# Column sums of an attention softmax: adding exponential tiles on VectorE ahead of the TensorE sums, in seven of 24 units

## The chip, the cores and the metric

The kernel runs on one core of a Trainium2 chip. Its time is the device time of one execution in microseconds (us); for the kernel before, the median of six runs is 421.89 us (420.82 to 422.49). The engines of the core are TensorE (PE in the profile, its weight loads PEld), VectorE (DVE), ScalarE (ACT), GpSimd (POOL) and SyncE (SP), which here only issues DMAs. Each engine works through its own queue in order and waits on semaphores.

## The reference

```python
def rmsnorm(x, g):
    return x / np.sqrt(np.mean(x * x, axis=-1, keepdims=True) + 1e-06) * g
q_n, k_n = rmsnorm(q, g_q), rmsnorm(k, g_k)          # (8, 12, 448, 64)
scores = (1 / sqrt(64)) * q_n @ k_n.T
attn = softmax(scores)                               # over 448 keys
x = (attn @ v) -> (8 * 448, 768)
h = x @ w_in                                         # (768, 2048)
out = np.maximum(0.01 * h, h) @ w_out                # (2048, 768), fp32
```

Eight batches of twelve heads are attended, and each of the 3584 tokens then passes a two-layer network with a leaky ReLU.

## The kernel before

The attention is done in 24 **units**; a unit is four heads of one batch, so three units make a batch. The four heads of a unit lie as two (`a`) by two (`r`) 64-wide blocks, so that four small matmuls fill the array together. The 448 keys of a unit are seven tiles of 64 (`NS = 7`). For each tile, `qk` (L198) computes the transposed scores with keys on the partitions, and `ex` (L205, its ScalarE row is L214) takes the exponential of 128 x 896 scores into `et[:, t]` in fp16.

A unit runs in four **stages** `d = 0..3` (L927 on) that treat the tiles (0), (1, 2), (3, 4), (5, 6). In each stage the scores and exponentials are issued first. Then comes `fill` (L702), which issues matmul items of the network from a queue, as many as the stage's share of the work allows, with small jobs between them: sums of squares (`prep_ssq`, L155), the norm's factor on ScalarE (`prep_rinv`, L160 and L161), the normalised q and k on VectorE (`prep_norm`, L167), and the DMA transpose of the unit after next (`prep_trd`). An item is 1.1 to 1.3 us of matmuls. The first layer (`moe1`, row L362) is evacuated by ScalarE (L356), the second (`moe2`, L403, and `seven`, L444) by VectorE (L407, L451, L460) with sums of activations on VectorE beside it (`s1` to `s4`, L425 to L434).

The softmax's denominators need a sum over keys, that is over partitions and over the seven tiles. TensorE makes it by matmuls with a matrix of ones, accumulating over the tiles in PSUM. From unit 4 to unit 22 (`narrow`, L696) this is `zcol` (L276): 28 matmuls with a 128 x 32 stationary matrix, 224 columns each, four side by side. The last unit uses `zsum_slot` (L268) with 28 matmuls of 64 x 64 by 448 columns. The sums of unit u - 1 are made in stage 0 of unit u, in this order on TensorE: score tile 0 of u, `pv` (values times exponentials) of u - 1, `zcol` of u - 1, `shift_mm` of u. `shift_mm` (L239) is a part of the maximum by which the exponentials are shifted: VectorE reduces tile 0 (L232), makes a diagonal `dg` (L234), TensorE spreads it (L244), VectorE reduces again (L245) and writes the bias `eb` (L253) that the first `ex` needs.

After `zcol`, ScalarE takes a logarithm (`zcol_ln`, L300) and an exponential of its negative (`zcol_inv`, L305), four DMAs on SP's queue broadcast the reciprocals into `rz` (L310), and the attention's result `x32`, copied from PSUM by ScalarE (`pv_out`, L295), is multiplied by `rz` into `xt` (L320). GpSimd does this product (`xmul_pool`) in stage 1 of the next unit, VectorE (`xmul_sb`) for units 4 to 6. `x32`, `rz` and `zs` have one buffer each. In the last unit the product of unit 22 stands in stage 2 on GpSimd, and after the loop come `zsum_slot`, `pv`, `zinv` (L326, L327, which also writes `rz`) and the product L349, then the last batch's network items.

The order on every engine is the order of the code (`manual_schedule`): nothing is rearranged.

Of the kernel before, what the change touches and what calls it, by code (L numbers as in the profile page):

```python
# [8 lines left out]
FP32 = mybir.dt.float32  # L9
FP16 = mybir.dt.float16  # L10
AF = mybir.ActivationFunctionType
ALU = mybir.AluOpType
# [6 lines left out]
def kernel(  # L19
# [11 lines left out]
    nc = tc.nc  # L31

    B, H, S, D = q.shape
    QH = 4
    NS = 7
    P = 128
    NQ = H // QH
    NU = B * NQ
# [6 lines left out]
    cst = ctx.enter_context(tc.tile_pool(name="cst", bufs=1))  # L45
# [4 lines left out]
    zpool = ctx.enter_context(tc.tile_pool(name="zpool", bufs=1))  # L50
# [6 lines left out]
    def aux(shape, dtype, name):  # L57
        if held:
            return held[0].pop(0)
        return psum.tile(shape, dtype, tag="aux", bufs=4, name=name)  # L60
# [6 lines left out]
    def drop(bank):  # L67
        if held:
            held[0].append(bank)
# [3 lines left out]
    ones16 = cst.tile([P, D], FP16)  # L73
    nc.vector.memset(ones16, 1.0)
    onesr = cst.tile([P, 32], FP16)
# [6 lines left out]
    nc.vector.memset(eps_t, 1.0e-6)  # L82
    one32 = cst.tile([1, 1], FP32)
    nc.vector.memset(one32, 1.0)
    grow = cst.tile([1, 2, D], FP32)
    gdup = cst.tile([1, 2, D], FP32)
    gcol = cst.tile([P, 1], FP32)
    gate_t = cst.tile([P, 1], FP16)
    vts = [cst.tile([P, 2, NS, D], FP16, name=f"vt{i}") for i in range(NV)]
# [21 lines left out]
    st = {}  # L111
# [77 lines left out]
    def slot():  # L189
        return psum.tile([P, 2, 512], FP32, tag="sT", bufs=2, name="sT")  # L190
# [7 lines left out]
    def qk(u, steps):  # L198
        st[u]["sT"] = []
        for t in steps:  # L200
            sT = slot()
            score(u, t, (sT[:, 0], sT[:, 1]))
            st[u]["sT"].append((t, sT))
# [17 lines left out]
    def shift_max(u):  # L221
        s = st[u]
        sT = s["sT"][0][1]
        if isinstance(sT, list):
            pm2 = small.tile([P, 2], FP32, tag="pm2", name="pm2")
            for a in range(2):
                nc.vector.tensor_reduce(pm2[:, a:a + 1], sT[a][:, 0:S], axis=AXL.X, op=ALU.max)
            s["spare"] = sT[0]
            nc.vector.tensor_reduce(s["spare"][:, 511:512], pm2, axis=AXL.X, op=ALU.max)
        else:  # L230
            s["spare"] = sT[:, 0]
            nc.vector.tensor_reduce(s["spare"][:, 511:512], sT[:, :, 0:S], axis=AXL.XY, op=ALU.max)  # L232
        s["dg"] = small.tile([P, P], FP16, tag="dg", name="dg")
        nc.vector.tensor_tensor(s["dg"], ident16, s["spare"][:, 511:512].broadcast_to([P, P]), op=ALU.mult)  # L234
# [20 lines left out]
    def gate(u):  # L255
        nc.gpsimd.tensor_copy(gate_t, buf(u, "n16")[:, 1, NS - 1, 1, D - 1:D])
# [3 lines left out]
    def zsum(u, t0=0, t1=NS):  # L260
        s = st[u]
        for t in range(t0, t1):
            for r in range(2):
                for a in range(2):
                    nc.tensor.matmul(s["zt"][r][64 * a:64 * a + 64, 0:S], ones16[64 * r:64 * r + 64],
                                     s["et"][64 * r:64 * r + 64, t, a], start=(t == 0), stop=(t == NS - 1))

    def zsum_slot(u):  # L268
        s = st[u]
        s["zslot"] = slot()  # L270
        s["zt"] = [s["zslot"][:, r] for r in range(2)]
        zsum(u)

    HS = S // 2

    def zcol(u):  # L276
        s = st[u]
        s["zc"] = aux([P, 512], FP32, "zc")
        for t in range(NS):
            for y in range(2):  # L280
                for a in range(2):
                    c = 32 * (2 * y + a)
                    nc.tensor.matmul(s["zc"][c:c + 32, 0:HS], onesr, s["et"][:, t, a, HS * y:HS * y + HS],  # L283
                                     start=(t == 0), stop=(t == NS - 1))

    def pv_slot(u):
        s = st[u]
        s["pslot"] = slot()
        s["pv"] = [s["pslot"][:, r] for r in range(2)]
        pv(u)  # L290

    def pv_out(u):
        s = st[u]
        s["x32"] = zpool.tile([P, 2, S], FP32, tag="x32", name="x32")
        nc.scalar.copy(s["x32"], s["pslot"][:, :, 0:S])  # L295

    def zcol_ln(u):
        s = st[u]
        s["zs"] = zpool.tile([P, HS], FP32, tag="zs", name="zs")
        nc.scalar.activation(s["zs"], s["zc"][:, 0:HS], AF.Ln)  # L300
        drop(s["zc"])

    def zcol_inv(u):
# [3 lines left out]
        for r in range(2):  # L307
            for y in range(2):
                src = s["zs"][64 * y + r:64 * y + 64:2, None, :]
                nc.sync.dma_start(s["rz"][:, r, HS * y:HS * y + HS], src.broadcast_to([32, 4, HS]))  # L310

    def xmul_sb(u):
        xmul_pool(u, nc.vector)

    def xmul_pool(u, eng=nc.gpsimd):
        s = st[u]
        b, g = divmod(u, NQ)
        if b not in xts:
            xts[b] = xpool.tile([P, NQ, 2, S], FP16, tag="xt", name="xt")
        eng.tensor_tensor(xts[b][:, g], s["x32"], s["rz"], op=ALU.mult)  # L320
# [375 lines left out]
    def narrow(u):  # L696
        return 4 <= u < NU - 1
# [46 lines left out]
    with tc.manual_schedule():  # L744
# [182 lines left out]
        for u in range(3, NU):  # L927
            for d in range(4):
                if d > 0 or u > 3:
                    qk(u, STEPS[d])  # L930
                    if d == 0:
                        shift_max(u)
                        if u == 6:
                            xmul_sb(u - 2)
                        if narrow(u - 1):
                            pv_slot(u - 1)
                            zcol(u - 1)
                            shift_mm(u)
                            pv_out(u - 1)
                        else:  # L940
                            zsum_slot(u - 1)
                            pv(u - 1)
                            shift_mm(u)
                            zinv(u - 1)
                    ex(u)
                    if d == 0 and narrow(u - 1):
                        zcol_ln(u - 1)
                jobs = []

                def job(fn, *args):  # L950
                    jobs.append(lambda: fn(*args))

                if d == 0:
                    if u == 3:
                        prep_norm(4)
                        gate(4)
                    elif narrow(u - 1):
                        if u < NU - 1:
                            job(zcol_inv, u - 1)
                    else:  # L960
                        xmul(u - 1)
                    if u + 4 < NU:
                        job(load, u + 4)
                    if u + 3 < NU:
                        load_v(u + 3)
                    if u < 6:
                        prep_sqp(u + 3)
                if d == 1 and narrow(u - 1) and not 5 <= u < 8 and u < NU - 1:
                    xmul_pool(u - 1)
                if u == NU - 1:  # L970
                    if d == 1:
                        job(zcol_inv, u - 1)
                    if d == 2:
                        xmul_pool(u - 1)
                if fed(u, d) and u > 3:
                    push(u // NQ - 1)
                if (u, d) in ((3, 1), (4, 0)):
                    for ti in range(2):
                        prep_tr(u + 1, ti, VV)
                if d == 1 and 5 <= u < NU - 1:  # L980
                    job(prep_g, u + 1)
                if u + 2 < NU:
                    if d == 1:
                        for ti in range(2):
                            job(prep_ssq, u + 2, ALL, (ti,))
                    if d == 2:
                        job(prep_rinv, u + 2)
                        for ti in range(2):
                            job(prep_norm, u + 2, ALL, (ti,))
                        if u > 3:  # L990
                            job(prep_trd, u + 2)
                if d == 1 and 4 <= u < 8:
                    job(weight_sum, u - 4, 0)
                if d == 0 and 5 <= u < 9:
                    job(weight_sum, u - 5, 1)
                if d == 2 and 6 <= u < 8:
                    job(xmul_sb, u - 1)
                if u == NU - 2 and d == 0:
                    for n, tile_ in ((1, (raws, "rq", 3)), (2, (raws, "rk", 3)), (3, None), (4, (prep_p, "sq", 3))):
                        job(win_sum, n, 1, tile_)  # L1000
                    for n in (3, 1, 2, 4):
                        job(x_sum, LATE, n)
                if d == 3 and 6 <= u < NU - 3:
                    for ti in range(2):
                        job(prep_sq, u + 3, ALL, (ti,))
                fill(u, d, jobs)
# [4 lines left out]
        for i, ns in enumerate(((3, 1), (2, 4))):  # L1011
            c, fn = queue[i]
# [33 lines left out]
```

## Time and profile before

| | |
|---|---|
| median of 6 runs | 421.89 us (420.82 to 422.49) |
| profiled execution | 421.53 us, of which the span is 419.8 us |
| granted TensorE clock | 0.994 |
| PE busy | 404.1 us, 96% |
| DVE busy | 270.6 us, 64% |
| ACT busy | 303.9 us, 72% |
| POOL busy | 83.0 us, 20% |
| sums of exponentials, L283 (19 units) | 15.4 us for 504 recorded matmuls |
| products `xt<-x,rz`, L320 | 16 on POOL, 2083 ns each; 3 on DVE, 1087 ns each |

The profile is of one execution. A row of its groups names line, engine, operation, tiles out<-in, shape, count, then the busy time with the mean of one in ns, and the idle time before them with what ended it. Matmuls that run side by side are each counted with their own duration, so the time of a group of them is read from the chain of waits or the timeline (start, duration, engine, line), not from the mean.

### The profile page before, as it was taken

Reading aid. Unit: us, or ns where it says so; the run is one execution under the profiler, and the core shown is the slowest. Engines: PE = TensorE matmul, PEld = TensorE weight load, DVE = VectorE, ACT = ScalarE, POOL = GpSimd, SP = SyncE. Lnnn points to the kernel's source line nnn. Section 1 sums busy time; section 2 is a strip of 40 time slices with the busy share of each in tenths; the row PEclk is TensorE's granted clock in tenths of the full one; section 3 lists DMA queues with packets and bytes.
Section 4 is the critical chain, followed back from the end, with each engine's and each line's share of the span. In section 5 each row is a group of like instructions: output and inputs, shape, how many; then the busy total and the mean of one; then the engine's idle time right before and its main releaser. Section 6 shows DMA issues by size and latency. Waiting matters only on the chain.

```text
span 419.8 us, 9568 instructions
## 1 busy us (share of the span) xinstructions
PE 404.1 (96%) x3959; PEld 222.6 (53%) x3959; DVE 270.6 (64%) x440; ACT 303.9 (72%) x474; POOL 83.0 (20%) x75
## 2 busy tenths in 40 slices
PE   7878999999999999999999999999999999999995
PEld 6544454455445444555455544455445557558863
DVE  5888675887668836566448735467338787527762
ACT  5999877768887689767986779967986657653600
POOL 1867432200020112210121121120101101010000
PEclk9899999999999999999999999999999999999999
DMA  7999999889764796678665796578552460032023
GB/s 268 216 239 241 238 250 147 210 153 212 151 155 81 205 206 134 164 167 179 154 135 98 200 202 146 155 140 165 185 108 44 121 157 9 8 76 75 2 53 99
DMA packets 71951, 62.42 MB, mean 149 GB/s; under 512 B 36324, under 2 KB 67044, under 8 KB 71908
## 3 DMA queue, kind: packets, MB, share of 16 engines
q1 hardware_dynamic: 61312, 49.62, 47.0%
q0 software_dynamic: 10272, 11.80, 18.1%
q8 instruction: 31, 0.51, 0.5%
q10 hardware_dynamic: 324, 0.39, 0.3%
q14 instruction: 12, 0.10, 0.1%
HBM read 45.61 MB, written 11.01 MB: 135 GB/s over the span
## 4 chain that ended last, share of the span: by engine, by line
PE 80%; ACT 9%; DVE 6%; issue 2%; DMA 1%; SPq 0%; DVEq 0%; ACTq 0%
PE hps L362 27%; PE sT L195 8%; ACT et L214 6%; PE sT L340 6%; PE ma L444 5%; PE bank L444 5%; PE md L444 5%; PE bank L564 4%; PE mc L444 4%; PE op L403 3%; PE zc L283 3%; PE mb L444 3%; DVE n L167 2%; PE sT L444 2%; PE bank L403 1%
## 5 line engine op out<-in xcount | busy, mean ns | idle before, releaser
L214 ACT ACTIVATE et<-sT,eb 128x896 f16<-128x896 f32 x166 | 159.6, 1011 | 18.5 <-PE sT L195 16.8
L362 PE MATMUL hps<-xt,win 128*128 128x448 f16 x600 | 120.8, 353 | 0.2 <-DVE xt L349 0.2
L362 PEld LDWEIGHTS <-win 128*128 128x128 f16 x612 | 56.8, 98 | 58.2 <-issue 9.6
L320 POOL TENSOR_TENSOR xt<-x,rz 128x896 f16<-128x896 f32 x16 | 33.3, 2083 | 149.7 <-DMA rz<-zs 141.8
L167 DVE TENSOR_TENSOR n<-rq,rinv 128x896 f16<-128x896 f32 (+2 forms) x25 | 28.5, 1143 | 49.4 <-ACT rinv L161 46.6
L356 ACT ACTIVATE gt<-hps 128x448 f16<-128x448 f32 x100 | 54.1, 557 | 5.9 <-PE hps L362 5.4
L195 PE MATMUL sT<-qkT 64*64 64x448 f16 x664 | 52.8, 366 | 3.3 <-ACT et L214 2.2
L155 DVE TENSOR_REDUCE ssq<-sq 128x14 f32<-128x896 f32 (+2 forms) x49 | 50.5, 1059 | 0.8 <-ACT sq L144 0.6
L444 PEld LDWEIGHTS <-sa 128*128 128x128 f16 x352 | 32.8, 98 | 26.3 <-issue 6.1
L295 ACT COPY x<-sT 128x896 f32<-128x896 f32 x19 | 17.2, 907 | 36.9 <-DVE sT L245 36.9
L124 POOL DMA_DIRECT2D vt<-in_v_dram x24 | 18.2, 759 | 113.8 <-PE sT L340 106.3
L444 PEld LDWEIGHTS <-gt 128*128 128x128 f16 x264 | 25.2, 98 | 19.4 <-issue 2.9
L195 PEld LDWEIGHTS <-qkT 64*64 64x64 f16 x672 | 15.3, 104 | 36.9 <-issue 33.0
L340 PE MATMUL sT<-et,vt 64*64 64x448 f16 x532 | 28.5, 349 | 0.3
L403 PE MATMUL op<-wout,gt 128*128 128x384 f16 x160 | 28.4, 327 | 0.0
L340 PEld LDWEIGHTS <-vt 64*64 64x64 f16 x672 | 20.6, 107 | 12.7 <-issue 1.7
L232 DVE TENSOR_REDUCE sT<-sT 128x1 f32<-128x896 f32 x22 | 24.0, 1093 | 3.5 <-PE sT L195 3.5
L167 DVE TENSOR_TENSOR n<-rk,rinv 128x896 f16<-128x896 f32 (+2 forms) x26 | 26.1, 1011 | 0.0
L403 PEld LDWEIGHTS <-gt 128*128 128x128 f16 x192 | 17.6, 98 | 14.3 <-issue 3.0
L444 PE MATMUL ma<-wout,gt 128*128 128x384 f16 x128 | 23.5, 326 | 0.0
L425 DVE TENSOR_TENSOR sa<-gt 128x512 f16<-128x512 f16 (+1 forms) x15 | 8.2, 545 | 18.5 <-ACT gt L356 13.8
L144 ACT ACTIVATE sq<-rq 128x896 f32<-128x896 f32 (+2 forms) x18 | 16.4, 914 | 1.3 <-DMA rq<-in_q_dram 1.3
(135 smaller groups left out, 516.4 us busy)
## 6 DMA issues: line engine op xcount, KB each, us to landing
rq<-in_q_dram SPq DMA_DIRECT2D x24, 448.0 KB, 3.9
rk<-in_k_dram SPq DMA_DIRECT2D x24, 448.0 KB, 5.7
out_dram<-ost SPq DMA_DIRECT2D x52, 192.0 KB, 3.6
rz<-zs SPq DMA_DIRECT2D x76, 112.0 KB, 2.3
vt<-in_v_dram POOLq DMA_DIRECT2D x24, 224.0 KB, 5.5
win<-in_moe_w_in_dram POOLq DMA_DIRECT2D x8, 384.0 KB, 16.1
wout<-in_moe_w_out_dram POOLq DMA_DIRECT2D x2, 1536.0 KB, 28.4
out_dram<-ost SPq DMA_DIRECT2D x4, 96.0 KB, 2.1
```

The lines of the kernel that those rows point to most:

```text
L124: nc.gpsimd.dma_start(vts[u % NV].rearrange("p a t d -> p a (t d)"), rows(v, u))
L155: nc.vector.tensor_reduce(buf(u, "ssq")[:, ti, :, c[0]:c[1]], buf(u, f"sq{ti}")[:, :, c[0]:c[1]], axis=AXL.X, op=ALU.add)
L167: nc.vector.tensor_tensor(buf(u, "n16")[:, ti, c[0]:c[1]].rearrange("p s a d -> p a s d"), src[:, :, c[0]:c[1]], buf(u, "rinv")[:, ti, :, ...
L195: nc.tensor.matmul(banks[a][64 * r:64 * r + 64, 0:S].rearrange("p (t x) -> p t x", t=NS), kT(u, r, a, t), qT(u, r, a), start=True, stop=True)
L214: nc.scalar.activation(s["et"][:, t], sT[:, :, 0:S], AF.Exp, bias=s["eb"], scale=1.0)
L232: nc.vector.tensor_reduce(s["spare"][:, 511:512], sT[:, :, 0:S], axis=AXL.XY, op=ALU.max)
L320: eng.tensor_tensor(xts[b][:, g], s["x32"], s["rz"], op=ALU.mult)
L340: nc.tensor.matmul(s["pv"][r][64 * a:64 * a + 64, 0:S], vts[u % NV][64 * r:64 * r + 64, a, t], s["et"][64 * r:64 * r + 64, t, a], start=(t ...
L356: nc.scalar.activation(dst, src, AF.Prelu, bias=0.0, scale=1.0, alpha=0.01)
L362: nc.tensor.matmul(hps[:, 0:S], win16[:, kt // 2, kt % 2, ts(ft, P)], xt[:, kt // 2, kt % 2], start=(kt == 0), stop=(kt == KT - 1))
L403: nc.tensor.matmul(op2[:, 0:HC], gt[:, ft, ds(col(t), P)], wout16[:, ft, ds(HC * half, HC)], start=(ft == 0), stop=(ft == FT - 1))
L444: nc.tensor.matmul(bank[:, 0:HC], a[:, f], b[:, f], start=(first and f == 0), stop=(f == HF - 1), skip_group_check=not first)
```

## The change

For units 10, 11, 13, 16, 17 and 19, VectorE adds the exponential tiles 0 to 3 into a new fp16 tile `ea` (three adds), in stage 2 right behind `ex`, and thus ahead of that stage's `fill`. `zcol` then sums tiles 4, 5, 6 and `ea`: 16 matmuls for 28. Behind the adds VectorE takes the product `xt<-x,rz` of the unit before, which GpSimd had in stage 1. For the last unit (23) VectorE adds tiles 0 to 4 (four adds) as a job of stage 3, followed there by the product of unit 22; `zsum_slot` sums tiles 5, 6 and `ea`: 12 matmuls for 28. The two rows of gains (`grow`, `gdup`) that are used only at the start move into the buffer of `x32`; `ea` has one buffer.

```diff
-    grow = cst.tile([1, 2, D], FP32)
-    gdup = cst.tile([1, 2, D], FP32)
+    g_t = zpool.tile([P, 2, S], FP32, tag="x32", name="g_t")
+    grow = g_t[0:1, 0, 0:2 * D].rearrange("p (a d) -> p a d", a=2)
+    gdup = g_t[0:1, 1, 0:2 * D].rearrange("p (a d) -> p a d", a=2)
...
-        zsum(u)
+        ets = z_tiles(u)
+        for i, e in enumerate(ets):
+            for r in range(2):
+                for a in range(2):
+                    nc.tensor.matmul(s["zt"][r][64 * a:64 * a + 64, 0:S], ones16[64 * r:64 * r + 64],
+                                     e[64 * r:64 * r + 64, a], start=(i == 0), stop=(i == len(ets) - 1))
...
+    ADDED = {u: 4 for u in (10, 11, 13, 16, 17, 19)}
+    ADDED[NU - 1] = 5
+
+    def add_e(u):
+        s = st[u]
+        s["ea"] = zpool.tile([P, 2, S], FP16, tag="ea", name="ea")
+        for t in range(1, ADDED[u]):
+            nc.vector.tensor_tensor(s["ea"], s["et"][:, 0] if t == 1 else s["ea"], s["et"][:, t], op=ALU.add)
+
+    def z_tiles(u):
+        s = st[u]
+        ets = [s["et"][:, t] for t in range(NS)]
+        return ets[ADDED[u]:] + [s["ea"]] if "ea" in s else ets
...
-        for t in range(NS):
+        ets = z_tiles(u)
+        for i, e in enumerate(ets):
...
-                    nc.tensor.matmul(s["zc"][c:c + 32, 0:HS], onesr, s["et"][:, t, a, HS * y:HS * y + HS],
-                                     start=(t == 0), stop=(t == NS - 1))
+                    nc.tensor.matmul(s["zc"][c:c + 32, 0:HS], onesr, e[:, a, HS * y:HS * y + HS],
+                                     start=(i == 0), stop=(i == len(ets) - 1))
...
+                if d == 2 and u in ADDED and u < NU - 1:
+                    add_e(u)
+                    xmul_sb(u - 1)
...
-                if d == 1 and narrow(u - 1) and not 5 <= u < 8 and u < NU - 1:
+                if d == 1 and narrow(u - 1) and not 5 <= u < 8 and u not in ADDED:
                     xmul_pool(u - 1)
...
-                    if d == 2:
-                        xmul_pool(u - 1)
...
+                if u == NU - 1 and d == 3:
+                    job(add_e, u)
+                    job(xmul_sb, u - 1)
```

## The prediction

> **What bounds the kernel.** I read three views in this order: the page's busy line and clock, the groups by shape, then the timeline around each place that the change touches.
>
> ```profile
> PE 404.1 (96%) x3959; PEld 222.6 (53%) x3959; DVE 270.6 (64%) x440; ACT 303.9 (72%) x474; POOL 83.0 (20%) x75
> ...
> PEclk9899999999999999999999999999999999999999
> ...
> PE 80%; ACT 9%; DVE 6%; issue 2%; DMA 1%; SPq 0%; DVEq 0%; ACTq 0%
> ```
>
> TensorE is busy 96% of the span at a full granted clock and carries 80% of the chain that ended last. So a microsecond taken off TensorE's queue counts, and one put on VectorE counts only where TensorE then waits for it. The changed units show no ACT or DVE piece in the chain, but for one exp pair in units 11 and 17 (at 173.59 and 269.49).
>
> **What the change removes.** From the instruction listings: 12 matmuls of `zcol` for each of units 10, 11, 13, 16, 17, 19 and 16 of the last `zsum_slot`, each with its weight load; seven GpSimd products. It adds 6 x 3 + 4 adds and seven products on VectorE. ScalarE and the DMAs keep their instructions and order.
>
> ```profile
> L283 PE MATMUL zc<-et,onesr 128*32 128x224 f16 x504 | 15.4, 261 | 0.0
> ...
> L428 DVE TENSOR_TENSOR sa<-sa,gt 128x1024 f16<-128x1024 f16 x7 | 4.8, 682 | 0.0
> ...
> L320 DVE TENSOR_TENSOR xt<-x,rz 128x896 f16<-128x896 f32 x3 | 3.3, 1087 | 0.0
> ```
>
> *Step 1, the column sums.* Four column groups run side by side, so the 261 ns of one matmul is no price. The chain of waits gives one `zcol` (7 tiles, 28 matmuls) 0.79 us up to the next group. In unit 10's (timeline, 161.75) the matmuls run 0.85 us to 162.60 and each takes 0.26, so the last four began at 162.34: six steps in 0.59, 0.098 a tile. The other 0.19 us, up to the following matmul at 162.53, is a foot that stays. Three tiles fewer are worth 3 x 0.098 = 0.295 us. Bounds: 0.28 (half the 0.187 a tile of the 448-wide groups, which take 1.32 for seven) and 0.34 (3/7 of 0.79). I take 0.295, the row itself.
>
> The Trainium skill (TensorEngine Tiling (Array Packing), Key Properties) speaks against counting 3/7 of the group: changing the tiling mode drains TensorE, however few matmuls stand between two changes. The 0.19 us foot agrees with it; 3/7 of 0.79 would give 0.27 us more over six groups than the foot allows.
>
> *Step 2, the matmul behind them.* After `zcol` TensorE runs `shift_mm`, which needs `dg` (L234) from VectorE. The shorter `zcol` is worth its time only if `dg` is done.
>
> ```profile
> 175.17 0.56 DVE L407 COPY ost<-op 128x384 f32<-128x384 f32 x1
> 175.65 0.69 DVE L428 TENSOR_TENSOR sa<-sa,gt 128x1024 f16<-128x1024 f16 x1
> 176.25 1.09 DVE L232 TENSOR_REDUCE sT<-sT 128x1 f32<-128x896 f32 x1
> 177.38 0.29 DVE L234 TENSOR_TENSOR dg<-ident,sT 128x128 f16<-128x128 f16 x1
> ```
>
> These are VectorE's rows (start, duration) around the sum of unit 11, which runs in unit 12, with `zcol` on TensorE from 177.00. `dg` ends at 177.67 and `shift_mm` starts at 177.79; with a wake-up of 0.05 only 0.07 us can be gained, and VectorE then sets it. Unit 17 is alike (`dg` ends 273.56, matmul 273.68). The others have room: unit 10 (162.13, 162.53), 13 (210.30, 210.80), 16 (257.93, 258.43), 19 (306.20, 306.69), at least 0.40 for 0.295. So 4 x 0.295 + 2 x 0.07 = 1.32 us. Bounds for the two: 0.05 and 0.34.
>
> *Step 3, the adds and products inside the units.* No row shows an add of 896 fp16 values with this layout. Between the groups of 672 (L550, 502 ns) and 1024 fp16 values (L428, 682 ns) it is 617 ns, an estimate; bounds 502, and 1087 from the product with fp32 inputs of this size. I take 0.62. The first two adds run in VectorE's gap while it waits for `rinv`; the third waits for the exp of tile 3, the first of a pair on ScalarE. Behind it in the queue stand the product (1.09) and `prep_norm`.
>
> ```profile
> 202.03 1.90 ACT L214 ACTIVATE et<-sT,eb 128x896 f16<-128x896 f32 x2
> ...
> 204.86 1.09 DVE L167 TENSOR_TENSOR n<-rq,rinv 128x896 f16<-128x896 f32 x1 [6.29 <-ACT rinv L161]
> ...
> 208.88 1.10 DVE L232 TENSOR_REDUCE sT<-sT 128x1 f32<-128x896 f32 x1 [0.46 <-PE sT L195]
> ```
>
> Unit 13: exp of tile 3 ends 202.03 + 1.01 = 203.04; add to 203.69; product to 204.78 (its `rz` landed by 201.83, when GpSimd started on it). The norm starts at 204.86 as before: 0.08 us to spare. The same sum gives 172.28 against 172.36 in unit 11, 253.54 against 253.62 in 16, 268.17 against 268.25 in 17, 300.68 against 300.75 in 19. So the cover is VectorE's wait for `rinv` (37.4 us over the middle of the trace). If it were gone, each 0.1 us late reaches L232; units 13 and 19 absorb 0.46 there, 16 absorbs 0.79, while 11 and 17 pass it all on. Cost taken: nothing. No PSUM evacuation stands behind the wait in units 10, 13, 16 and 19 (`hps` goes to ScalarE); in 11 and 17 one does, L407, after the norms.
>
> ```profile
> 156.77 2.07 POOL L320 TENSOR_TENSOR xt<-x,rz 128x896 f16<-128x896 f32 x1 [8.51 <-DMA rz<-zs]
> ...
> 157.73 2.07 DVE L167 TENSOR_TENSOR n<-rq,rinv 128x896 f16<-128x896 f32 x1 [6.20 <-ACT rinv L161]
> ```
>
> Unit 10 is the exception: `rz` lands at 156.77, so the product ends at 157.86 and the norm starts 0.13 late. But its 2.07 us here, against 1.09 elsewhere, ran beside GpSimd's product, which is now gone; the two norms end near 159.95 instead of 160.80, ahead of the score at 160.61. Nothing on the path.
>
> The Trainium skill (SBUF — State Buffer, Who interferes with whom) says that a VectorE instruction with two SBUF inputs contends with a GpSimd instruction that reads SBUF. The doubled row agrees. By it the change takes a collision away and makes none, as GpSimd has no product in these units; in the sum neither moves TensorE.
>
> The moved product has readers only three or more stages later (`push` of its batch), and frees `x32` and `rz` two stages before they are written again. SP's `rz` transfers and ScalarE's copy now wait for VectorE in GpSimd's place, long after; GpSimd's queue only empties.
>
> *Step 4, the last unit.*
>
> ```profile
> 370.88 0.56 DVE L451 TENSOR_TENSOR ost<-bank,ost 128x384 f32<-128x384 f32 x1 [0.74 <-PE bank L444]
> 374.09 0.56 DVE L451 TENSOR_TENSOR ost<-bank,ost 128x384 f32<-128x384 f32 x1 [2.65 <-PE bank L444]
> ```
>
> Seven tiles of 64x64 sums (`zsum_slot`, L265, 374.05 to 375.50 in the chain) become three: 4 x 0.187 = 0.75 us (bounds 0.56, three tiles' worth, and 4/7 of 1.45 = 0.83). The listing puts the adds behind the first of these two VectorE rows, in the idle stretch of 2.65 us before the second: 371.47 + 4 x 0.62 + 3 x 0.04 = 374.07. TensorE first takes tiles 5 and 6 (374.05 to 374.42) and so has the sum in time, by 0.35. The product then runs to 375.16; L326 writes its `rz` buffer and waits for it, so it starts at 375.2 instead of 375.60 (L326's row), gaining 0.4 where TensorE gains 0.75. VectorE's chain of L349 and L550 rows up to 381.4 is then 0.35 late against TensorE; the matmul that needs it first, at 382.97, has 1 us of room. Full 0.75.
>
> **Sum.** 1.32 + 0.75 = 2.07 us. The profiled execution took 421.53 us (span 419.8 and 1.7 around it): 419.46. It lies 0.36 under the median of the runs, 421.89; on that scale the forecast is **419.8 us**, 0.5% faster. With the bounds of steps 1 and 4 and the runs' spread its own range is 419.2 to 420.6. (A measurement here can tell about 0.2% from no change: 421.05 and 422.73.)
>
> **Rivals.**
>
> *B, everything counts:* `dg` comes earlier in units 12 and 18 too and the foot shrinks with the group: 6 x 0.34 + 0.83 = 2.87, 419.0. For it: L232 is only third in a row of VectorE work there. Against it: L407 ahead of it waits for TensorE itself.
>
> *C, fp16 adds at the fp32 rate (1.09 each):* norms 0.4 late. Units 13, 16 and 19 absorb it, 10 too (4 x 0.295 gained); 11 and 17 lose 0.28 each; in the last unit the sum ends at 375.95, TensorE waits and ends 0.8 later. -1.18 + 0.56 + 0.8 = +0.2: 422.1, no change. Against it: all fp16 rows from SBUF run at half the fp32 price.
>
> *D, slower, VectorE becomes the bound at the change of unit:* the moved product takes 2.07 instead of 1.09, as the one collided norm did. Place: in front of `prep_norm` in the stage of tiles 3 and 4. It is then 0.9 late: `dg` of units 12 and 18 comes at 178.54 and TensorE loses 0.80 each; 13 and 19 keep 0.03 of their gain, 10 keeps 0.12, 16 all; in the last unit L326 starts 0.65 later than before and TensorE later waits 0.5, leaving 0.25. 1.60 - 0.06 - 0.12 - 0.295 - 0.25 = +0.9: 422.8. It decides from about 0.5 us of lateness. Against it: GpSimd has nothing to read then.
>
> **Chances.** Forecast 0.62, B 0.15, C 0.12, D 0.11. Faster by over 0.2% is A and B, 0.77; within it C, 0.12; slower D, 0.11. The range 418.8 to 421.9 takes in A, B and the milder half of C.
>
> **What would show it.** Right: `zcol` pieces near 0.50 us in six units; `ea` adds near 0.62; norms of the six units still released by `rinv`; `shift_mm` of units 12 and 18 starting right behind `dg`; L265 near 0.56. Wrong: norms starting after VectorE's own product, a TensorE wait for `ea` in the last sum, or adds near 1.09. A VectorE row other than `dg` in front of TensorE in units 10 to 20 would break step 3.

## The result and the profile after

The changed kernel takes 419.89 us (median of 17 runs, 419.01 to 422.45) against 421.93 of the kernel before (36 runs): a ratio of 0.9956, 95% interval 0.9946 to 0.9967. The forecast was 419.8. Its profiled execution took 419.89 us, 1.64 less than that of before, with a span of 418.1.

Line numbers shift in the changed kernel: by 1 up to the sums and by 20 behind them (21 in the experiments on the last unit's product), so that the product L320 is L340 there, L349 is L369 and L407 is L427. The adds are L288.

On the page of the changed kernel, the busy line and the chain by engine:

```profile
PE 400.7 (96%) x3871; PEld 220.3 (53%) x3871; DVE 290.1 (69%) x469; ACT 303.9 (73%) x474; POOL 68.5 (16%) x68
...
PE 79%; ACT 9%; DVE 8%; issue 2%; DMA 1%; SPq 0%; DVEq 0%; ACTq 0%
```

The reader sees 88 matmuls fewer on PE, 19.5 us more work on DVE, 14.5 us less on POOL, and a chain that has gained 2% of DVE. The new pieces of VectorE in the chain stand at three places: from L427 to `dg` at the sums of units 11 and 17 (175.12 to 177.62 and 270.35 to 272.85), and at L369 and L471 in the last unit (376.08 to 377.72).

VectorE in unit 11 of the changed kernel (start, duration, engine, line, then the idle time before it and who ended it):

```profile
170.50 0.63 DVE L288 TENSOR_TENSOR ea<-ea,et 128x896 f16<-128x896 f16 x1 [1.32 <-ACT et L215]
171.04 1.08 DVE L340 TENSOR_TENSOR xt<-x,rz 128x896 f16<-128x896 f32 x1
172.30 1.09 DVE L168 TENSOR_TENSOR n<-rq,rinv 128x896 f16<-128x896 f32 x1 [0.17 <-ACT rinv L162]
```

The last add waits 1.32 us for its exponential, the product follows, and the norm is still released by `rinv` after 0.17 us of waiting. So the work lies inside the old gap. In five of the six units the norm waits 0.17 us; in unit 17 the product waits 0.24 us for its `rz` and the norm follows it at once, released by VectorE's own product and no longer by `rinv`.

TensorE at the sums of the same unit:

```profile
176.94 0.47 PE L303 MATMUL zc<-et,onesr 128*32 128x224 f16 x12
177.24 0.27 PE L303 MATMUL zc<-ea,onesr 128*32 128x224 f16 x4
177.66 0.22 PE L245 MATMUL sT<-dg,onesp 128*128 128x64 f16 x2
```

VectorE just ahead of it:

```profile
175.12 0.56 DVE L427 COPY ost<-op 128x384 f32<-128x384 f32 x1
175.59 0.68 DVE L448 TENSOR_TENSOR sa<-sa,gt 128x1024 f16<-128x1024 f16 x1
176.19 1.09 DVE L233 TENSOR_REDUCE sT<-sT 128x1 f32<-128x896 f32 x1
177.32 0.29 DVE L235 TENSOR_TENSOR dg<-ident,sT 128x128 f16<-128x128 f16 x1
```

`dg` ran from 177.32 to 177.61, so `shift_mm` started 0.05 us behind it and 0.42 behind the start of the last tile. In unit 10 this last distance is 0.20, which is the foot of 0.19 seen before:

```profile
162.28 0.27 PE L303 MATMUL zc<-ea,onesr 128*32 128x224 f16 x4
162.48 0.23 PE L245 MATMUL sT<-dg,onesp 128*128 128x64 f16 x2
```

To compare kernels stage by stage I take the time from one start of `shift_mm` on TensorE to the next, each time from the stage 0 of a unit to that of the following one, from the timelines. The units from 12 to 21 that are not listed agree within 0.02 us in these five kernels.

| from `shift_mm` of unit to the next, us | before | change | adds only | product twice | s2 later |
|---|---|---|---|---|---|
| 10 | 14.62 | 14.35 | 14.34 | 14.34 | 14.34 |
| 11 | 15.26 | 15.18 | 15.43 | 15.83 | 14.97 |
| 13 | 16.90 | 16.61 | 16.61 | 16.77 | 16.61 |
| 16 | 15.93 | 15.65 | 15.64 | 15.64 | 15.64 |
| 17 | 15.25 | 15.18 | 15.60 | 16.06 | 14.97 |
| 19 | 16.89 | 16.61 | 16.61 | 16.79 | 16.61 |
| gained in the six | | 1.27 | 0.62 | -0.58 | 1.71 |
| last unit, sums to `pv` | 1.35 | 0.60 | 1.12 | 0.59 | 0.59 |
| `pv` to the last batch's first matmul | 5.34 | 5.57 | 5.36 | 5.57 | 5.57 |

The change gains 1.27 in the six units and 0.75 - 0.23 = 0.52 in the last, 1.79 us in all, in the middle of what the ratio's interval allows (1.4 to 2.3 us). The 1.64 us between the two profiled executions is this less some 0.2 us by which the changed kernel's was already late when the first changed unit began (`shift_mm` at 148.13 against 147.91). That start says nothing of the change: in the eight kernels here that have the same code up to there it lies between 147.32 and 148.88, which is why single executions are compared by stage.

### The profile page after: what moved, and what is told of

Read it like the earlier page. It is cut to its first block, busy times and chain, and to the rows that moved or that the text cites. A ratio compares the mean times of both kernels' runs of the same rounds, so it can differ in the third digit from the quotient of the medians.

```text
span 418.1 us, 9413 instructions
## 1 busy us (share of the span) xinstructions
PE 400.7 (96%) x3871; PEld 220.3 (53%) x3871; DVE 290.1 (69%) x469; ACT 303.9 (73%) x474; POOL 68.5 (16%) x68
## 4 chain that ended last, share of the span: by engine, by line
PE 79%; ACT 9%; DVE 8%; issue 2%; DMA 1%; SPq 0%; DVEq 0%; ACTq 0%
PE hps L382 27%; PE sT L196 8%; PE sT L360 5%; PE ma L464 5%; ACT et L215 5%; PE md L464 5%; PE bank L584 4%; PE mc L464 4%; PE bank L464 4%; PE op L423 4%; PE mb L464 3%; PE zc L303 3%; DVE n L168 2%; PE sT L464 2%; PE bank L423 1%
## 5 line engine op out<-in xcount | busy, mean ns | idle before, releaser
L168 DVE TENSOR_TENSOR n<-rq,rinv 128x896 f16<-128x896 f32 (+2 forms) x25 | 27.4, 1098 | 13.8 <-ACT rinv L162 11.0
L340 POOL TENSOR_TENSOR xt<-x,rz 128x896 f16<-128x896 f32 x9 | 19.0, 2116 | 81.4 <-DMA rz<-zs 81.4
L288 DVE TENSOR_TENSOR ea<-ea,et 128x896 f16<-128x896 f16 x15 | 9.4, 626 | 13.6 <-ACT et L215 13.3
```

The lines of the kernel that those rows point to most:

```text
L168: nc.vector.tensor_tensor(buf(u, "n16")[:, ti, c[0]:c[1]].rearrange("p s a d -> p a s d"), src[:, :, c[0]:c[1]], buf(u, "rinv")[:, ti, :, ...
```

## The experiments

The theory: the gain is TensorE's removed matmuls, as far as VectorE's rows do not take their place. The rivals: GpSimd's relief is the gain; TensorE's count alone decides.

| | time, us | ratio to before | 95% interval |
|---|---|---|---|
| the change | 419.89 | 0.9956 | 0.9946 to 0.9967 |
| products only | 421.68 | 0.9996 | 0.9981 to 1.0011 |
| adds only | 421.11 | 0.9974 | 0.9960 to 0.9988 |
| six units only | 420.43 | 0.9962 | 0.9949 to 0.9974 |
| last unit only | 421.48 | 0.9989 | 0.9976 to 1.0001 |
| product twice | 421.44 | 0.9998 | 0.9985 to 1.0012 |
| twelve units | 427.85 | 1.0161 | 1.0131 to 1.0191 |
| s2 later | 419.34 | 0.9938 | 0.9925 to 0.9951 |
| product first | 419.68 | 0.9953 | 0.9940 to 0.9965 |
| both repairs | 418.86 | 0.9938 | 0.9926 to 0.9950 |
| s2 later, no adds | 421.38 | 1.0005 | 0.9991 to 1.0019 |

Each ratio is to runs of the kernel before on the same chip.

**Products only.** The adds go, the moved products stay.

```diff
-                    add_e(u)
                     xmul_sb(u - 1)
...
-                    job(add_e, u)
                     job(xmul_sb, u - 1)
```

> The seven products go to VectorE as in the change, but nothing is added: TensorE keeps all its column-sum matmuls. Theory (the gain is TensorE's removed matmuls): none of the 2.07 us, 421.9 us, ratio 1.000, between 0.998 and 1.002; unit 10's norm falls from 2.07 to 1.09 us and nobody gains by it. Rival (the gain is GpSimd's relief, its products no longer beside VectorE's): most of the 2 us, 420.0 us, ratio 0.9955.

No gain: 0.9996. The collision in unit 10 is gone, as the norm's row in the timeline shows:

```profile
157.46 1.09 DVE L168 TENSOR_TENSOR n<-rq,rinv 128x896 f16<-128x896 f32 x1
```

It took 2.07 us before. VectorE then waits 0.79 us for the score, so nobody needed the 0.98. GpSimd's relief as such is worth nothing that the interval (0.9981 to 1.0011) can tell, nor is the move of `grow` and `gdup`, which this kernel has too.

**Adds only.** The adds stay, the products go back to GpSimd.

```diff
                     add_e(u)
-                    xmul_sb(u - 1)
...
-                if d == 1 and narrow(u - 1) and not 5 <= u < 8 and u not in ADDED:
+                if d == 1 and narrow(u - 1) and not 5 <= u < 8 and u < NU - 1:
                     xmul_pool(u - 1)
...
+                    if d == 2:
+                        xmul_pool(u - 1)
...
                     job(add_e, u)
-                    job(xmul_sb, u - 1)
```

> The adds of the change without its products: GpSimd keeps all 16, so they run at about 2.1 us beside VectorE's work again. Theory: the six units keep 1.3 us, the last unit keeps 0.75, and the last L326 no longer waits for VectorE's product, so that the 0.25 us lost behind it comes back, unless GpSimd's product slows the adds beside it: 419.5 to 420.1 us, ratio 0.9945 to 0.9960. Rival (GpSimd's relief is the gain): 421.9, ratio 1.000. Second rival (the product was moved because it collides with the adds on the path): 420.8 or more.

0.9974: neither my range nor the first rival, but the second, which gives the collision as the reason. In unit 11 GpSimd's product runs from 169.48 to 171.55, and VectorE's third add runs beside it:

```profile
169.48 2.07 POOL L340 TENSOR_TENSOR xt<-x,rz 128x896 f16<-128x896 f32 x1 [7.17 <-DMA rz<-zs]
...
169.69 2.34 DVE L288 TENSOR_TENSOR ea<-ea,et 128x896 f16<-128x896 f16 x1 [1.27 <-ACT et L215]
```

Alone the add takes 0.63. It ends at 172.03, 0.48 after the product: it hardly moved while the product ran. The norm starts at 171.96, behind the add instead of at `rinv`, and unit 11 is 0.17 us longer than before. In unit 17, 0.35 us longer, it is the norm that collides (1.72 us for 1.09). In units 10, 13, 16 and 19 rows collide too, but the table shows `shift_mm` no later there than in the change. In the last unit the first of the four adds takes 1.32 beside GpSimd's product, and TensorE waits for the sum:

```profile
372.74 0.57 PE L277 MATMUL sT<-et,ones 64*64 64x448 f16 x8
373.67 0.38 PE L277 MATMUL sT<-ea,ones 64*64 64x448 f16 x4 [0.36 <-DVE ea L288]
```

The two starts lie 0.93 apart, 0.41 in the change. So the product's move is no gain by itself but what lets the adds pay: with it 1.79 us, without it 0.62 + 0.23 - 0.02 = 0.83.

The Trainium skill (SBUF — State Buffer, Who interferes with whom) has the rule: a VectorE instruction with two SBUF inputs contends with a GpSimd instruction that reads SBUF. These rows agree, and give the price.

**Six units only** and **last unit only.** Each keeps one half of `ADDED`.

```diff
-    ADDED[NU - 1] = 5
```
```diff
-    ADDED = {u: 4 for u in (10, 11, 13, 16, 17, 19)}
+    ADDED = {}
```

> The change in units 10, 11, 13, 16, 17, 19 alone; the last unit as before. Theory: 4 x 0.295 + 2 x 0.07 = 1.3 us, 420.6 us, ratio 0.997; the matmul of shift_mm comes 0.28 earlier after the sums of units 10, 13, 16 and 19 and 0.07 after 11 and 17. Rival (every unit gives its three tiles): 6 x 0.34 = 2.0 us, 419.9, ratio 0.995.

> The change in the last unit alone. Theory: TensorE saves 0.75 us in the sum and loses 0.25 behind it, where the last md matmuls wait for a VectorE row that stands behind the product that waits for the reciprocal: 0.5 us net, 421.4 us, ratio 0.9988. Rival (the last unit gives 0.75 whole): 421.15, ratio 0.9982; in the trace, no TensorE gap behind the second item after the sum.

0.9962 and 0.9989. The interval of the second reaches 1.0001, so by its time alone it isn't clear that the last unit gains. In the timelines the six units gain the same 0.27, 0.08, 0.29, 0.28, 0.07 and 0.28 without the last, and the last has its 0.59 and 5.57 us without the six: the parts add up.

**Product twice.** The six units take the moved product a second time, with the same operands and result.

```diff
                     add_e(u)
                     xmul_sb(u - 1)
+                    xmul_sb(u - 1)
```

> In the six units VectorE takes the moved product twice, to the same tile: 1.0 us more behind the third add. Theory (VectorE's wait for rinv covers the work with 0.1 to 0.2 us to spare, and what exceeds it passes to dg): norms start about 0.85 us later in all six; units 11 and 17 lose 0.85 each, 13 and 19 have 0.46 ahead of L232 and little behind, lose their 0.28 and a little more, 10 and 16 lose little; in all 2.3 to 3.2 us against the change: 422.2 to 423.1, ratio 1.000 to 1.003. Rival (VectorE at 69% busy has room anyway): 419.9, ratio 0.9956.

0.9998, so 1.8 us are lost to 1.0 us more of VectorE in six places; 421.44 lies below my 422.2 to 423.1. Unit 11 on TensorE:

```profile
177.77 0.22 PE L245 MATMUL sT<-dg,onesp 128*128 128x64 f16 x2 [0.80 <-DVE dg L235]
```

TensorE waits for `dg`, which shows the cover and who is late when it is gone. Against the change, unit 17 loses 0.88 and 11 loses 0.65, 13 and 19 0.16 and 0.18, 10 and 16 nothing. I had overlooked that L407 (now L427) in 11 and 17 waits for TensorE itself: in unit 11 the norm is 0.87 later against the third add, L427 only 0.66, since in the change it starts 0.81 behind the start of the row ahead of it and here 0.60. In unit 17, where the change had left no cover, the two are 1.02 and 0.89.

**Twelve units.** The change in every unit from 10 to 21, and the last.

```diff
-    ADDED = {u: 4 for u in (10, 11, 13, 16, 17, 19)}
+    ADDED = {u: 4 for u in range(10, 22)}
```

> The change in all twelve units from 10 to 21 and the last: six more sets of three adds and a product, in units whose stage 2 or 3 has second-layer work of VectorE. Theory (only a gap pays): units 12, 14, 15, 18, 20 and 21 have VectorE rows back to back up to L232, so that some 1 to 2 us of the 2.95 reach TensorE in each, against 0.3 gained: 4 to 10 us slower than the change, 424 to 430. Rival (TensorE's matmuls are what counts, and VectorE has room on average): 6 x 0.295 more gained, 418.1, ratio 0.991.

1.0161, 6 us slower than before. Units 12 and 18 are 1.0 us longer than before, 14 and 20 2.6, 15 0.5 and 21 0.2. VectorE and TensorE in unit 14:

```profile
221.85 1.08 DVE L340 TENSOR_TENSOR xt<-x,rz 128x896 f16<-128x896 f32 x1
222.86 0.55 DVE L480 COPY ost<-ma 128x384 f32<-128x384 f32 x1
```
```profile
223.46 1.46 PE L464 MATMUL ma<-wout,gt 128*128 128x384 f16 x8 [2.73 <-DVE ost L480]
```

The evacuation of `ma` stands behind the adds and the product, and the next matmuls into that bank wait 2.73 us for it. With VectorE at 64% on average before, it is the gap at this place that decides.

**s2 later.** In the even batches the 0.68 us row L428 (`s2`) is issued one item later, behind L232.

```diff
-                std[1] = also(std[1], lambda: later(s2, tt))
-                std[2] = also(std[2], lambda: later(s3, tt), lambda: later(s4, tt))
+                std[2] = also(std[2], lambda: later(s2, tt), lambda: later(s3, tt), lambda: later(s4, tt))
```

> As the change, with s2 (the 0.68 us row L428) one item later in the even batches, so that it no longer stands ahead of L232 in units 12 and 18. Theory (there dg sets TensorE after the shorter sums): dg 0.6 us earlier, each of the two units gains the missing 0.22 us: 419.45, ratio 0.9945; shift_mm right behind the column sums. Rival (dg does not decide): 419.9, ratio 0.9956, and shift_mm where it was.

0.9938. Units 11 and 17 now take 14.97 us, 0.21 less each, and TensorE has no wait left behind the sums:

```profile
177.34 0.27 PE L303 MATMUL zc<-ea,onesr 128*32 128x224 f16 x4
177.54 0.23 PE L245 MATMUL sT<-dg,onesp 128*128 128x64 f16 x2
```

0.20 from one to the other, the foot alone, as in unit 10.

**s2 later, no adds.** The same edit on the kernel before.

> The kernel before, no adds and products where they were, with s2 one item later in the even batches. Theory (dg decides only behind the shortened sums; in the kernel before it was done 0.12 us ahead of its matmul): nothing, 421.9 us, ratio 0.999 to 1.001, and shift_mm of units 12 and 18 directly behind the column sums as before. Rival (s2 later is worth 0.4 us for another reason): 421.4, ratio 0.999 or below, with a gain in other units.

1.0005, and units 11 and 17 at 15.25 and 15.25 us. The row order is worth something only once the sums are short; this is the change's own lost part.

**Product first.** In the last unit the product of unit 22 and two of the four adds are taken in stage 2, between second-layer rows.

```diff
-                if u == NU - 1 and d == 3:
-                    job(add_e, u)
+                if u == NU - 1 and d == 2:
+                    job(flush)
+                    job(add_e, u, 1, 3)
                     job(xmul_sb, u - 1)
+                if u == NU - 1 and d == 3:
+                    job(add_e, u, 3, 5)
```

> As the change, but in the last unit two adds and the product of unit 22 are taken in stage 2, between the second-layer rows, and only two adds in stage 3, so that the rz buffer is free before the last sums end. Theory (the lost 0.25 us is L326 waiting for the product, which makes the md rows late): L326 starts right behind the sums, 0.4 us earlier, the TensorE gap behind the second item goes: 0.25 us less than the change, 419.65, ratio 0.995. Rival (the gap has another cause): 419.9 and the gap stays.

The question is the 0.23 us after the last `pv`. TensorE of the change, where the third item starts 1.55 us after the second instead of 1.30:

```profile
373.48 1.49 PE L360 MATMUL bank<-et,vt 64*64 64x448 f16 x28
374.90 1.47 PE L464 MATMUL bank<-tw,sa 128*128 128x384 f16 x8
376.21 1.46 PE L464 MATMUL bank<-wout,sa 128*128 128x384 f16 x8
377.76 1.46 PE L464 MATMUL bank<-tw,gt 128*128 128x384 f16 x8
```

VectorE of the change at that time:

```profile
376.08 1.16 DVE L369 TENSOR_TENSOR xt<-bank,rz 128x448 f16<-128x448 f32 x2 [1.55 <-ACT rz L347]
377.15 0.55 DVE L471 TENSOR_TENSOR ost<-bank,ost 128x384 f32<-128x384 f32 x1
```

The third item accumulates into the PSUM bank that L471 reads (`md`), L471 ends at 377.70, and it stands behind L369, which waits for the reciprocal. The rows of the change that come before (the last sums, the product of unit 22, and ScalarE's row):

```profile
373.29 0.36 PE L277 MATMUL sT<-ea,ones 64*64 64x448 f16 x4
...
372.98 1.09 DVE L340 TENSOR_TENSOR xt<-x,rz 128x896 f16<-128x896 f32 x1
...
374.15 0.92 ACT L346 ACTIVATE rz<-sT 128x896 f32<-128x896 f32 x1 [1.76 <-PE sT L277]
```

The profile puts this wait down to TensorE's sums, but they ended near 373.65, 0.5 us earlier; the product of unit 22 held `rz` until 374.07. With the product first, ScalarE begins 0.41 behind the start of the last tile's matmuls (373.45 to 373.86) instead of 0.86, and TensorE runs through:

```profile
373.86 0.92 ACT L347 ACTIVATE rz<-sT 128x896 f32<-128x896 f32 x1 [1.31 <-PE sT L277]
...
375.06 1.47 PE L465 MATMUL bank<-tw,sa 128*128 128x384 f16 x8
376.37 1.46 PE L465 MATMUL bank<-wout,sa 128*128 128x384 f16 x8
377.67 1.46 PE L465 MATMUL bank<-tw,gt 128*128 128x384 f16 x8
```

`pv` to the last batch takes 5.33 us, 0.24 less. 0.9953 is as expected but no separate proof; the timeline carries this verdict.

**Both repairs.** The edits of s2 later and of product first, together.

> The change with both repairs: s2 later, and in the last unit the product and two adds in stage 2. Theory (the two losses are separate): 0.42 and 0.24 us come off the change's time, 419.2 us, ratio 0.9938. Rival (s2 later delays the last unit's rows and eats the second repair): 419.4, ratio 0.9945.

418.86 us, 0.9938: faster than the kernel before, and by the timelines than the change: units 11 and 17 take 14.97 and 14.96 us, `pv` to the last batch 5.34, so 0.66 us less. The two ratios' intervals touch (0.9946 to 0.9950), and the two kernels were not timed against each other, so by time alone this order isn't settled. The ratio is also that of s2 later alone, so the second repair's 0.24 us is seen in the timelines only.

## Why the prediction was right

*Step 1, three tiles 0.295 us.* Measured 0.27, 0.29, 0.28 and 0.28 in units 10, 13, 16 and 19. The foot stayed (0.20), so 3/7 of the group (0.34) would have been too much.

*Step 2, 0.07 us in units 11 and 17.* Measured 0.08 and 0.07, with `shift_mm` 0.05 us behind `dg`. The s2 experiment shows the cause, and the same edit without the adds shows that nothing else in it pays.

*Step 3, adds hidden.* The adds took 617 to 627 ns (most of them 624 to 626) against 617 estimated; in five of the six units the norm was still released by `rinv`, with 0.17 us to spare where I had 0.08, as the product starts 0.1 us before the add's recorded end. In unit 17 it was not: the four transfers of `rz` were issued over 3.77 us instead of 2.53 (why stays open), and the norm stood behind VectorE's own product, one of my signs of being wrong. It cost nothing there, as L427 still started 0.04 us behind the end of TensorE's `op` matmuls. What the cover is worth was right in kind and too dear in units 11 and 17: I had them pass on all lateness, and of 0.87 and 1.02 us they passed on 0.65 and 0.88, by the wait of L407. That GpSimd's relief is nothing on the path was right, but I did not see that leaving the product there would have cost about 1 us.

*Step 4, the last unit 0.75 us whole.* This is the step that failed. The sums did shorten by 0.75 and `ea` was ready in time (L340 starts at 372.98, the `ea` matmuls at 373.29). But I named as first reader of VectorE's late chain the matmul of 382.97, "1 us of room", and overlooked the `md` add within that chain, whose bank TensorE needs at 377.5. VectorE's chain was about as late as forecast: L369 started 2.60 us behind the first `pv` matmul, where L349 had started 2.20 behind it before. But the `md` add had only 0.2 us of room (before, L451 ended at 379.16 and the third item began at 379.37). 0.52 came out, and product first gives the rest back.

The sum was 2.07 us, the timelines show 1.79: 0.23 less from step 4 and 0.06 less from step 1. By the timelines the forecast would have been 420.1; that the median came within 0.1 us of 419.8 is in part luck, as the ratio's interval leaves 1.4 to 2.3 us open. Of the rivals, B fails by steps 1 and 2, C by the adds' 625 ns, and D's doubled row appears only where the product stays on GpSimd.

## What to carry to other kernels

Work moved from a full engine to one with idle time pays only where the gap is: name the instruction that waits there, what it waits for, and what stands behind the new work in the queue up to the next row that the full engine needs. After shortening one group on the full engine, look at what it waits for next, since a neighbour that was just in time (0.12 us here) sets the end. When two engines can do the moved product, ask which of them runs beside the new work.

## What the runs showed of the hardware

Beside a GpSimd product of two fp32 SBUF tiles, a VectorE add of two fp16 SBUF tiles took 2.34 us instead of 0.63, and 1.32 in the last unit, while the GpSimd product kept its 2.07 and 2.09 us. I had expected a slower add, not one that all but stands still until the other ends. All five adds of that run that began while a product ran (units 11, 13, 16, 19 and the last; 1.28 to 2.34 us long) ended 0.48 us after it, whenever they had begun, and two norms (1.90 us in unit 10, 1.72 in 17, 1.09 alone) 0.94 and 0.95 us after it. So the time lost was what was left of the product, less about 0.15 us. In every one of these pairs the product had begun first.
